# A fused kernel's last stage by 512 tokens, with its output products five feature blocks behind

## The chip, the core and the metric

The program runs on one core of a Trainium2 chip. Five engines work in it, each through its own list of instructions in a fixed order: TensorE (PE, matmuls; PEld are its weight loads), VectorE (DVE), ScalarE (ACT), GpSimd (POOL) and SyncE (SP, which issues every DMA of this kernel). They wait for one another through semaphores. The metric is the device time of one execution, in microseconds. Before the change it is 1073.4 us (median of three runs, 1073.21 to 1075.92).

## What is computed

All inputs are float32, drawn with numpy (several arrive as float64 words and are decoded on the chip). Cut to what matters:

```python
# attention with a compressive memory, B, H, S, D = 4, 8, 576, 64
out = g * mem_out + (1 - g) * softmax(causal(q @ k.T / 8)) @ v
x = out.transpose(0, 2, 1, 3).reshape(2304, 512)
# first layer, 512 -> 2048 -> 512
h = x @ w_in
x = (h * tanh(log1p(exp(h)))) @ w_out
# second layer, 512 -> 1024 -> 1024 -> 512
a = x @ w1
b = x @ w2
result = (a * b @ w3) @ w_out2
```

## The kernel before

Every large product is kept near float32 precision by splitting each operand into a rounded high part and a low remainder and adding three products (high by high, high by low, low by high). So one logical product of a 128-row block is three matmuls per 128 rows of depth.

There are three parts. In the first, 16 pairs of heads go through attention. In the second, the first layer runs by quarters of its 2048 features (g = 0 to 3, in the code `emit_h` and `emit_x2`), each over eight units of 288 tokens; `x2` collects the result. While the quarters run, the weights of the second layer are decoded from their 64-bit words by `decode` (six DVE operations and one POOL addition per 128x512 block) and parked in DRAM. In the last quarter `fold()` multiplies w3 by w_out2 once, so that the second layer's two last products become one: for each of 8 row blocks it takes two half steps; a half step loads raw words (`draw`), decodes them into `da`, transposes them on PE (four 128x128 transposes, L597), has ACT and DVE split the transposed block into `w3h` and `w3l`, and adds twelve 128x512 matmuls in a `psF` bank. After the second half step ACT and DVE write the block out through `da` and `de`, and two DMAs put it in `w_dram` (L611, L612).

The third part is the stage that the change rewrites. It takes `x2` by 256 tokens (`T`), nine chunks. For each chunk, `emit_ab` does eight feature blocks: 12 matmuls for b, 12 for a, then ACT, DVE, ACT and DVE turn them into the split product of a and b in `pbuf`. `emit_out` of the chunk before follows: two blocks of 128 tokens, each 24 matmuls of 512 columns against the folded weight `wft`, an ACT copy and a DMA to the output. `wft` is read back from `w_dram` into the place of `o2` once the fold is done.

Two things set the order. The code emits fold steps between units by `steps(folding, 3)`, and a scheduler then orders the instructions of each engine by priority of emission and by its own timing, so that what is ready early fills gaps. Tiles of one tag share a fixed number of buffers, and a new tile gets its buffer when the old one's last reader is done; the eight PSUM banks are three `A`, three `X`, two `F`. The fold uses both `F` banks, one for the sum and one for the transposes. In the quarters `gh` and `gl` are the split activations that `emit_x2` reads.

Of the kernel before, what the change touches and what calls it, by code (L numbers as in the profile page):

```python
# [21 lines left out]
def fused_kernel(ctx: ExitStack, tc, q, k, v, M_prev, z_prev, beta, w_in, w_out, w1, w2, w3, w_out2, out):  # L22
# [23 lines left out]
    def psA():  # L46
        return bank("A")
# [35 lines left out]
    def decoder(stack, raw, n):  # L83
        dec.update(pool=stack.enter_context(tc.tile_pool(name="dec", bufs=1)), raw=raw, n=n)
# [369 lines left out]
    def emit_h(u):  # L454

        g, b, z = u
        t = wts[g]
        x = xl[b]
        cs = slice(CH * z, CH * z + CH)
        y = [wps[0].tile([128, 2, CH], F32, tag=f"y{i}", name="y", bufs=1) for i in range(2)]  # L460
        hp = []
        for m in range(KQ):
            o = bank(HU.get(u, HT[g == NQ - 1])[m])[:, 0:CH]
            ms = slice(128 * m, 128 * m + 128)
            for kk in range(KD):
                mm(o, t[:, 0, kk, ms], x[:, 0, kk, cs], kk == 0, False)
                mm(o, t[:, 0, kk, ms], x[:, 1, kk, cs], False, False)
                mm(o, t[:, 1, kk, ms], x[:, 0, kk, cs], False, kk == KD - 1)
            hp.append(o)
        for m in range(KQ):  # L470
            nc.scalar.activation(out=y[m // 2][:, m % 2], in_=hp[m], func=AF.Tanh, scale=0.5)

        d = wps[0].tile([128, 1], F32, tag="dum", name="dum", bufs=2)
        first = nc.scalar.activation(out=d, in_=y[1][:, 1, 0:1], func=AF.Sin, scale=0.0)
        with tc.issue_after(first.ins):
            for i in range(2):
                nc.scalar.activation(out=y[i], in_=y[i], func=AF.Arctan, scale=-0.5, bias=half)
        gg = []
        for i in range(2):
            nc.scalar.activation(out=y[i], in_=y[i], func=AF.Sin, scale=-2.0, bias=halfpi)  # L480
            for j in range(2):
                nc.vector.tensor_tensor(out=y[i][:, j], in0=y[i][:, j], in1=hp[2 * i + j], op=ALU.mult)
            gh = wps[0].tile([128, 2, CH], F32R, tag="gh", name="gh", bufs=3)
            gl = wps[0].tile([128, 2, CH], F32R, tag="gl", name="gl", bufs=3)
            nc.scalar.copy(out=gh, in_=y[i])
            sub(gl, y[i], gh)
            gg.append((gh, gl))
        gt[u] = gg
# [133 lines left out]
    folding = fold()  # L622
    nextq = iter(())
    prev = None
    w1t, w2t, wft = [None, None], [None, None], [None]
    for u in [(g, b, z) for g in range(NQ) for b in range(B) for z in range(2)]:
        g, b, z = u
        last = g == NQ - 1
        if u not in gt:
            if last and fpool[0] is None:  # L630
                steps(nextq, 100)
                steps(pre, 100)
                dk.close()
                fpool[0] = fk.enter_context(tc.tile_pool(name="fp", bufs=1))
                decoder(fk, 1, 2)
            emit_h(u)
        if last:
            if z == 0 and b > 0:
                wt, wd = ((w1t, w1_dram), (w2t, w2_dram))[(b - 1) % 2]
                i = (b - 1) // 2  # L640
                wt[i] = w_slot(b - 1, "w12t")
                from_dram(wt[i], wd, slice(512 * i, 512 * i + 512))
            if b > 0:
                steps(folding, 3)
        if prev is not None:
            emit_x2(prev)
        if not last:
            if b == 0 and z == 0:
                nextq = load_quarter(g + 1)
            steps(nextq, 2)  # L650
            steps(pre, 1)
        prev = u
# [6 lines left out]


    wp3 = ctx.enter_context(tc.tile_pool(name="wp3", bufs=1, side="right"))
    T = 256
    NM = FF2 // 128
    pp = {}
    late = [None]
    pbuf = w2q[0].tile([128, 2, 2, NM, T], F32R, tag="wq1", name="pbuf")

    def emit_ab(c):
        xh = wp3.tile([128, KD, T], F32R, tag=f"x2h{c % 2}", name="x2h", bufs=1)
        xlo = (wp3 if c % 2 == 0 or c < 3 else late[0]).tile([128, KD, T], F32R, tag="x2l", name="x2l", bufs=1)  # L670
        s = x2[:, :, T * c:T * c + T]
        nc.scalar.copy(out=xh, in_=s)
        sub(xlo, s, xh)
        t = pbuf[:, c % 2]
        pp[c] = t
        for m in range(NM):
            pa, pb = psA()[:, 0:T], psA()[:, 0:T]
            m2 = slice(128 * (m % 4), 128 * (m % 4) + 128)
            for o, w, cs in ((pb, w2t[m // 4], m2), (pa, w1t[m // 4], m2)):
                for kk in range(KD):  # L680
                    mm(o, w[:, 0, kk, cs], xh[:, kk], kk == 0, False)
                    mm(o, w[:, 0, kk, cs], xlo[:, kk], False, False)
                    mm(o, w[:, 1, kk, cs], xh[:, kk], False, kk == KD - 1)
            bs = wp3.tile([128, T], F32, tag="bs", name="bs", bufs=2)
            nc.scalar.copy(out=bs, in_=pb)
            nc.vector.tensor_tensor(out=bs, in0=bs, in1=pa, op=ALU.mult)  # L686
            nc.scalar.copy(out=t[:, 0, m], in_=bs)  # L687
            sub(t[:, 1, m], bs, t[:, 0, m])
            if c < 2:
                steps(folding, 1)  # L690

    def emit_out(c):
        t = pp.pop(c)
        for i in range(T // 128):
            o = psX()
            ts = slice(128 * i, 128 * i + 128)
            for m in range(NM):
                w = wft[0][:, :, 4 * (m // 4):4 * (m // 4) + 4]
                mm(o, t[:, 0, m, ts], w[:, 0, m % 4], m == 0, False)
                mm(o, t[:, 0, m, ts], w[:, 1, m % 4], False, False)  # L700
                mm(o, t[:, 1, m, ts], w[:, 0, m % 4], False, m == NM - 1)
            ob = wp3.tile([128, DM], F32, tag="ob", name="ob", bufs=2)
            nc.scalar.copy(out=ob, in_=o)
            r0 = T * c + 128 * i
            dm(out=out[r0:r0 + 128, :], in_=ob)

    NC = NT // T
    for c in range(NC):
        emit_ab(c)
        if c == 1:  # L710
            steps(folding, 100)
            fk.close()
            late[0] = ctx.enter_context(tc.tile_pool(name="late", bufs=1))
            wft[0] = wq.tile([128, 2, NM, DM], F32R, tag="wq0", name="wft")
            for i in range(2):
                for s in range(2):
                    dm(
                        out=f(wft[0][:, i, 4 * s:4 * s + 4]),
                        in_=w_dram[i, 512 * s:512 * s + 512, :].rearrange("(k p) f -> p k f", p=128),
                    )  # L720
        if c > 0:
            emit_out(c - 1)
    emit_out(NC - 1)


# [30 lines left out]
```

## Time and profile before

| | |
|---|---|
| Median of the runs | 1073.4 us |
| The profiled execution: its own time / its span | 1075.49 us / 1073.7 us |
| PE busy | 1023.7 us, 95% |
| DVE, ACT, POOL busy | 63%, 51%, 36% |
| Mean granted clock of PE | 0.991 of full speed |
| Chain of work that ended last | PE 62%, DVE 20%, POOL 7%, DMA 6% |

The span is what the profiler saw of one execution; the execution's own time lies 1.8 us above it. An engine's busy share is an average over very different parts. PE is idle for some 34 us in the first 300 us, and close to always busy after that; so in the rest of the program a stretch of time is worth what PE has to do in it, plus what PE waits. In timeline rows the columns are start, length, engine, line, operation, output and inputs with their sizes, the count and, in brackets, the idle time before it and who ended it. Lengths of matmuls overlap, since they are pipelined: the pace is read from starts, or from a long run of them.

### The profile page before, as it was taken

How to read it: one execution, taken by the hardware profiler on the slowest of the kernel's cores; microseconds unless marked ns; L12 is line 12 of the kernel's file. 1: busy time of each engine (PE TensorE's matmuls, PEld its weight loads, DVE VectorE, ACT ScalarE, POOL GpSimd, SP SyncE). 2: the span in 40 equal slices, each digit the busy share in tenths (PEclk: the TensorE clock that was granted, in tenths of full speed). 3: DMA queues.
4: the chain of work that ended last, by engine and by line, in shares of the span. 5: the costliest groups of instructions: out<-in, count | busy, mean ns of one | idle time of the engine just before them, and what ended most of it. 6: DMA issues, size and time to landing. Idle time of an engine off the chain costs nothing.

```text
span 1073.7 us, 19071 instructions
## 1 busy us (share of the span) xinstructions
PE 1023.7 (95%) x7128; PEld 913.2 (85%) x7128; DVE 671.9 (63%) x1563; ACT 548.0 (51%) x1157; POOL 387.3 (36%) x377
## 2 busy tenths in 40 slices
PE   6998898899998999999999999999999999999998
PEld 5665655567798999999999999999998999999997
DVE  6699999896689888888987535647551122222220
ACT  5776767677765666666666655653231222222221
POOL 7668898784255556555555001010100000000000
PEclk9999999999999999999999999999999999999999
DMA  6788777675233343333332264323115100000001
GB/s 149 167 188 188 186 181 184 169 187 117 79 98 101 112 161 109 109 130 127 118 99 101 63 243 146 136 89 128 62 58 176 40 5 17 20 21 16 6 20 40
DMA packets 111341, 116.70 MB, mean 109 GB/s; under 512 B 71696, under 2 KB 73744, under 8 KB 111248
## 3 DMA queue, kind: packets, MB, share of 16 engines
q1 hardware_dynamic: 111248, 115.48, 37.6%
q8 instruction: 56, 0.92, 0.4%
q14 instruction: 37, 0.30, 0.1%
HBM read 71.83 MB, written 21.50 MB: 87 GB/s over the span
## 4 chain that ended last, share of the span: by engine, by line
PE 62%; DVE 20%; POOL 7%; DMA 6%; issue 3%; SPq 1%; ACT 0%; DVEq 0%; POOLq 0%; ACTq 0%
PE psA L59 28%; PE psX L59 24%; PE psF L59 6%; DVE de L104 3%; POOL da L120 2%; DVE da L102 2%; PE psF L426 2%; DVE de L103 2%; DVE s L361 2%; DVE da L99 2%; POOL da L105 2%; DVE da L98 2%; DVE da L100 2%; DMA w_dram<-da 1%; DVE s L356 1%
## 5 line engine op out<-in xcount | busy, mean ns | idle before, releaser
L105 POOL TENSOR_TENSOR da<-da,de 128x512 f32<-128x512 f32 x72 | 100.1, 1395 | 336.0 <-DVE de L104 272.6
L59 PE MATMUL psX<-gh,wqt 128*128 128x288 f32 x1024 | 209.0, 298 | 9.9 <-DVE x L575 5.4
L59 PE MATMUL psA<-x2h,w12t 128*128 128x256 f32 x1152 | 210.4, 283 | 0.0
L59 PEld LDWEIGHTS psA<-x2h,w12t 128*128 128x128 f32 x1152 | 180.8, 192 | 1.0
L59 PEld LDWEIGHTS psX<-gh,wqt 128*128 128x128 f32 x1024 | 164.6, 188 | 13.5 <-DVE x L575 6.7
L59 PE MATMUL psA<-x2l,w12t 128*128 128x256 f32 x576 | 163.2, 284 | 0.4 <-DVE x2l L65 0.4
L59 PE MATMUL psX<-gl,wqt 128*128 128x288 f32 x512 | 150.9, 295 | 0.0
L686 DVE TENSOR_TENSOR bs<-bs,psA 128x256 f32<-128x256 f32 x72 | 30.3, 421 | 161.5 <-PE psA L59 156.8
L59 PE MATMUL psA<-xt,wqt 128*128 128x288 f32 x840 | 119.9, 296 | 0.0
L59 PEld LDWEIGHTS psA<-xt,wqt 128*128 128x128 f32 x840 | 115.0, 189 | 2.3 <-issue 1.0
L59 PEld LDWEIGHTS psA<-x2l,w12t 128*128 128x128 f32 x576 | 110.3, 192 | 1.4 <-DVE x2l L65 0.7
L366 ACT ACTIVATE s<-s,acc 128x512 f32<-128x512 f32 (+4 forms) x144 | 84.2, 587 | 39.7 <-DVE acc L361 34.2
L59 PE MATMUL psX<-wft,pbuf 128*128 128x512 f32 x432 | 101.7, 394 | 2.3 <-DMA wft<-w_dram 2.3
L59 PEld LDWEIGHTS psX<-wft,pbuf 128*128 128x128 f32 x432 | 81.4, 190 | 19.3 <-DMA wft<-w_dram 2.8
L59 PEld LDWEIGHTS psX<-gl,wqt 128*128 128x128 f32 x512 | 96.5, 189 | 0.2
L687 ACT CAST pbuf<-bs 128x256 fp32r<-128x256 f32 x72 | 29.3, 406 | 110.4 <-DVE bs L686 97.3
L98 DVE TENSOR_SCALAR da<-draw 128x512 int32<-128x512 int32 x72 | 44.1, 616 | 61.5 <-DMA draw<-in_moe_w_dram 23.1
L59 PE MATMUL psF<-xt,wqt 128*128 128x288 f32 x552 | 77.3, 295 | 0.0
L426 PE MATMUL psF<-ident,s 128*128 128x128 f32 x400 | 67.7, 283 | 10.0 <-DVE s L356 6.6
L59 PE MATMUL psX<-pt,raw 128*64 128x64 f32 (+4 forms) x576 | 74.8, 329 | 0.0
L59 PEld LDWEIGHTS psF<-xt,wqt 128*128 128x128 f32 x552 | 74.5, 188 | 0.1
L361 DVE CUSTOM_DVE_ANT_0 s<-psA,mask 128x512 f32<-128x512 f32 (+3 forms) x144 | 64.2, 477 | 15.0 <-PE psA L59 11.0
(116 smaller groups left out, 1920.8 us busy)
## 6 DMA issues: line engine op xcount, KB each, us to landing
draw<-in_moe_w_dram SPq DMA_DIRECT2D x32, 512.0 KB, 3.7
draw<-in_moe_w_out_dram SPq DMA_DIRECT2D x24, 512.0 KB, 3.9
draw<-in_moe_w_in_dram SPq DMA_DIRECT2D x16, 512.0 KB, 4.4
w12t<-w_dram SPq DMA_DIRECT2D x8, 1024.0 KB, 7.8
w_dram<-de SPq DMA_DIRECT2D x24, 256.0 KB, 2.4
w_dram<-da SPq DMA_DIRECT2D x24, 256.0 KB, 2.4
out_dram<-ob SPq DMA_DIRECT2D x18, 256.0 KB, 2.0
eqk<-hl SPq DMA_DIRECT2D x30, 144.0 KB, 2.7
```

The lines of the kernel that those rows point to most:

```text
L59: nc.tensor.matmul(o, lhsT=l, rhs=r, start=start, stop=stop)
L98: V.tensor_scalar(out=ai, in0=hw, scalar1=0x7FFFFFFF, scalar2=None, op0=ALU.bitwise_and)
L99: V.tensor_scalar(out=a, in0=a, scalar1=2.0 ** -15, scalar2=122879.9921875, op0=ALU.max, op1=ALU.min)
L100: V.tensor_scalar(out=ai, in0=ai, scalar1=3, scalar2=0x3FFFFFF8, op0=ALU.logical_shift_left, op1=ALU.bitwise_and)
L102: V.scalar_tensor_tensor(out=ai, in0=hw, scalar=-0x40000000, in1=ai, op0=ALU.bitwise_and, op1=ALU.bitwise_or)
L104: V.scalar_tensor_tensor(out=e, in0=lw.bitcast(U32), scalar=2.0 ** -52, in1=e, op0=ALU.mult, op1=ALU.mult)
L105: nc.gpsimd.tensor_tensor(out=a, in0=a, in1=e, op=ALU.add)
L361: nc.vector.tensor_tensor_reduce(out=s, in0=o, in1=m, op0=ALU.add, op1=ALU.min, scale=-scale, scalar=init, accum_out=a,)
L366: nc.scalar.activation(out=s, in_=s, func=AF.Exp, scale=-1.0, bias=a, accum_out=r)
L426: nc.tensor.transpose(o[:, 128 * x:128 * x + 128], src[:, 128 * jb:128 * jb + 128], ident)
L686: nc.vector.tensor_tensor(out=bs, in0=bs, in1=pa, op=ALU.mult)
L687: nc.scalar.copy(out=t[:, 0, m], in_=bs)
```

## The change

The last stage takes 512 tokens at a time (four spans of 512 and one of 256). One feature block of `emit_ab` is now 24 matmuls of 512 columns. Its bank for a is `A` in even blocks and `F` in odd ones. The output products come one feature block at a time, five blocks behind (`LAG`), and add into four banks that stay open over a whole span (`X`, `X`, `X`, `F`). The products of a and b go through a ring of six blocks instead of `pbuf`. The fold gets two raw buffers in place of one, its steps begin one unit earlier in the last quarter, and the code asks for one more step in each of the first five blocks. `gh` and `gl` have two buffers in place of three. `wft` is loaded with the first 512 rows of both parts first.

```diff
-            gh = wps[0].tile([128, 2, CH], F32R, tag="gh", name="gh", bufs=3)
-            gl = wps[0].tile([128, 2, CH], F32R, tag="gl", name="gl", bufs=3)
+            gh = wps[0].tile([128, 2, CH], F32R, tag="gh", name="gh", bufs=2)
+            gl = wps[0].tile([128, 2, CH], F32R, tag="gl", name="gl", bufs=2)
...
-                decoder(fk, 1, 2)
+                decoder(fk, 2, 2)
...
-            if b > 0:
+            if (b, z) > (0, 0):
                 steps(folding, 3)
...
-    T = 256
+    T = 512
+    RING = 6
...
+    def emit_ab(k):
+        c, m = work[k]
+        n = spans[c][1]
+        x = xs_[c % 2]
+        pb, pa = (bank(t)[:, 0:n] for t in ("AA", "AF")[m % 2])
+        m2 = slice(128 * (m % 4), 128 * (m % 4) + 128)
+        for o, w in ((pb, w2t[m // 4]), (pa, w1t[m // 4])):
+            for kk in range(KD):
+                mm(o, w[:, 0, kk, m2], x[0][:, kk, 0:n], kk == 0, False)
+                mm(o, w[:, 0, kk, m2], x[1][:, kk, 0:n], False, False)
+                mm(o, w[:, 1, kk, m2], x[0][:, kk, 0:n], False, kk == KD - 1)
+        t = ring[:, k % RING]
+        bs = wp3.tile([128, T], F32, tag="bs", name="bs", bufs=1)[:, 0:n]
...
+        if m == 0:
+            outs[c] = [bank(tag) for tag in "XXXF"[0:n // 128]]
+        for i, o in enumerate(outs[c]):
+            ts = slice(128 * i, 128 * i + 128)
+            mm(o, t[:, 0, ts], wft[0][:, 0, m], m == 0, False)
+            mm(o, t[:, 0, ts], wft[0][:, 1, m], False, False)
+            mm(o, t[:, 1, ts], wft[0][:, 0, m], False, m == NM - 1)
...
+    LAG = RING - 1
+    split_x2(0)
+    for k, (c, m) in enumerate(work):
+        emit_ab(k)
+        if k < LAG:
+            steps(folding, 1)
+        if k == LAG - 1:
+            end_fold()
+        if m == 5 and c + 1 < len(spans):
+            split_x2(c + 1)
+        if k >= LAG:
+            emit_out(k - LAG)
```

How the instructions move is seen at three places. The first is PE in the fold's last part, before: `ident,da` is the name of a half step's transposes (they stand above this piece), `o,w3h` and `o,w3l` its products, `x2h` and `x2l` blocks of the last stage.

```order
L59 MATMUL psA<-x2l,w12t 128x256
L59 MATMUL psA<-x2h,w12t 128x256 x2
L59 MATMUL psA<-x2l,w12t 128x256
L59 MATMUL psA<-x2h,w12t 128x256 x2
L59 MATMUL psF<-o_7976,w3h 128x512 x2
L59 MATMUL psA<-x2l,w12t 128x256
L59 MATMUL psA<-x2h,w12t 128x256 x2
L59 MATMUL psA<-x2l,w12t 128x256
L59 MATMUL psA<-x2h,w12t 128x256
L59 MATMUL psF<-o_7976,w3l 128x512
L59 MATMUL psF<-o_7976,w3h 128x512 x2
```

Between the transposes and the first product stand 26 matmuls of the last stage, and five or more between the first products with `w3h` and the first with `w3l`. The same engine and place in the changed kernel (`room` holds the low part of x2):

```order
L59 MATMUL psA<-room,w12t 128x512
L59 MATMUL psA<-x2h,w12t 128x512
L597 MATMUL psF<-ident,da 128x128 x4
L59 MATMUL psF<-o_7841,w3h 128x512 x2
L59 MATMUL psF<-o_7841,w3l 128x512
L59 MATMUL psF<-o_7841,w3h 128x512 x2
L59 MATMUL psF<-o_7841,w3l 128x512
L59 MATMUL psF<-o_7841,w3h 128x512 x2
L59 MATMUL psF<-o_7841,w3l 128x512
L59 MATMUL psF<-o_7841,w3h 128x512 x2
L59 MATMUL psF<-o_7841,w3l 128x512
L597 MATMUL psF<-ident,da 128x128 x4
```

The last four of the 16 half steps now stand one straight behind another, with nothing of the last stage between; the 72 matmuls that the three `A` banks can take stand ahead of them, and 36 more with `F` banks behind them.

The second place is DVE at the same stretch. Before, the last half step's words are decoded like this (`bs`, `pbuf` belong to the last stage):

```order
L98 TENSOR_SCALAR da_9179<-draw_9177 128x512
L99 TENSOR_SCALAR da_9179<-da_9179 128x512
L100 TENSOR_SCALAR da_9179<-da_9179 128x512
L102 SCALAR_TENSOR_TENSOR da_9179<-draw_9177,da_9179 128x512
L686 TENSOR_TENSOR bs_9803<-bs_9803,psA_9777 128x256
L65 TENSOR_TENSOR w3l_9025<-psF_9026,w3h_9024 128x512
L103 TENSOR_SCALAR de_9180<-da_9179 128x512
L65 TENSOR_TENSOR pbuf_9334<-bs_9803,pbuf_9334 128x256
L104 SCALAR_TENSOR_TENSOR de_9180<-draw_9177,de_9180 128x512
```

And in the changed kernel, from the split of the last but two half step (`w3l_8851`) on; `de_8872` writes out row block 6, `da_8880` and `da_9047` are the words of the last two half steps:

```order
L65 TENSOR_TENSOR w3l_8851<-psF_8852,w3h_8850 128x512
L98 TENSOR_SCALAR da_8880<-draw_8878 128x512
L99 TENSOR_SCALAR da_8880<-da_8880 128x512
L610 TENSOR_TENSOR de_8872<-psF_8806,da_8871 128x512
L100 TENSOR_SCALAR da_8880<-da_8880 128x512
L102 SCALAR_TENSOR_TENSOR da_8880<-draw_8878,da_8880 128x512
L98 TENSOR_SCALAR da_9047<-draw_9045 128x512
L103 TENSOR_SCALAR de_8881<-da_8880 128x512
L99 TENSOR_SCALAR da_9047<-da_9047 128x512
L104 SCALAR_TENSOR_TENSOR de_8881<-draw_8878,de_8881 128x512
L100 TENSOR_SCALAR da_9047<-da_9047 128x512
```

Two half steps are decoded in turn now. The writing out of block 6 stands inside the decoding of `da_8880`, and so does the first operation on `da_9047`, whose buffer is the one that `da_8871` leaves when its DMA to DRAM is done.

The third place is DVE in quarter 1, one unit of 288 tokens, before (`x2` with `psX` is what `emit_x2` adds up, `gl` the low part of the activations):

```order
L577 TENSOR_TENSOR x2_3941<-x2_3941,psX_6318 128x288
L482 TENSOR_TENSOR y_6229<-y_6229,psF_6256 128x288
L482 TENSOR_TENSOR y_6229<-y_6229,psF_6269 128x288
L65 TENSOR_TENSOR gl_6294<-y_6228,gh_6293 128x576
L577 TENSOR_TENSOR x2_3941<-x2_3941,psX_6332 128x288
L65 TENSOR_TENSOR gl_6301<-y_6229,gh_6300 128x576
L577 TENSOR_TENSOR x2_3941<-x2_3941,psX_6346 128x288
```

and after:

```order
L577 TENSOR_TENSOR x2_3941<-x2_3941,psX_6318 128x288
L482 TENSOR_TENSOR y_6229<-y_6229,psF_6256 128x288
L482 TENSOR_TENSOR y_6229<-y_6229,psF_6269 128x288
L577 TENSOR_TENSOR x2_3941<-x2_3941,psX_6332 128x288
L98 TENSOR_SCALAR da_6510<-draw_6508 128x512
L99 TENSOR_SCALAR da_6510<-da_6510 128x512
L65 TENSOR_TENSOR gl_6294<-y_6228,gh_6293 128x576
L577 TENSOR_TENSOR x2_3941<-x2_3941,psX_6346 128x288
```

The first `gl` moved behind the third addition into x2, and the second behind the fourth, into the stretch of decoding that stands ahead of the next unit's first addition.

## Rows read from the trace of the kernel before

**Rows 1.** The page: busy us (share) xinstructions, and PE's granted clock in 40 slices.

```profile
PE 1023.7 (95%) x7128; PEld 913.2 (85%) x7128; DVE 671.9 (63%) x1563; ACT 548.0 (51%) x1157; POOL 387.3 (36%) x377
...
PEclk9999999999999999999999999999999999999999
```

**Rows 2.** PE's waits from 730 to 860: us in total, times, longest us.

```profile
PE psX L59 <- DMA wft<-w_dram: 2.3, 1, 2.3
PE psA L59 <- DVE x2l L65: 0.4, 1, 0.4
```

**Rows 3.** The chain that ended last: start us, us, what; one chunk.

```profile
855.54 23.03 PE psA L59 x192
878.58 10.91 PE psX L59 x48
```

**Rows 4.** Timeline of PE behind its wait for the folded weight.

```profile
819.75 9.20 PE L59 MATMUL psX<-wft,pbuf 128*128 128x512 f32 x33 [2.35 <-DMA wft<-w_dram]
```

**Rows 5.** Windows of 1 us: busy by engine, granted clock, DMA share, GB/s.

```profile
819.00:820.00 1.00, 0.25 (x1) 0.25 (x2) 0.00 (x0) 0.00 (x0) 0.00 (x0) 0.72 0.98 375
...
822.00:823.00 1.00, 1.00 (x4) 0.77 (x3) 0.00 (x0) 0.00 (x0) 0.00 (x0) 0.57 0.75 231
```

**Rows 6.** Timeline, one half step of the fold and its writing out.

```profile
735.46 0.60 PE L597 MATMUL psF<-ident,da 128*128 128x128 f32 x4
735.82 0.38 PE L59 MATMUL psX<-gh,wqt 128*128 128x288 f32 x1
736.10 0.59 ACT L599 CAST w3h<-psF 128x512 fp32r<-128x512 f32 x1 [7.44 <-PE psF L597]
736.73 0.68 DVE L65 TENSOR_TENSOR w3l<-psF,w3h 128x512 fp32r<-128x512 f32 x1
737.76 0.63 PE L59 MATMUL psF<-o,w3h 128*128 128x512 f32 x2
740.52 0.52 PE L59 MATMUL psA<-x2h,w12t 128*128 128x256 f32 x3
740.77 0.59 ACT L609 CAST da<-psF 128x512 fp32r<-128x512 f32 x1 [0.81 <-issue]
```

**Rows 7.** Timeline, decoding of a block on DVE and POOL.

```profile
748.30 0.43 DVE L98 TENSOR_SCALAR da<-draw 128x512 int32<-128x512 int32 x1 [0.43 <-DMA draw<-in_moe_w_dram]
748.76 0.43 DVE L99 TENSOR_SCALAR da<-da 128x512 f32<-128x512 f32 x1
751.90 0.69 DVE L104 SCALAR_TENSOR_TENSOR de<-draw,de 128x512 f32<-128x512 uint32 x1
752.72 1.30 POOL L105 TENSOR_TENSOR da<-da,de 128x512 f32<-128x512 f32 x1 [6.42 <-issue]
```

**Rows 8.** DMA issues from 735 to 850: KB each, median us to landing.

```profile
w_dram<-da SPq DMA_DIRECT2D x4, 256.0 KB, 2.2
```

**Rows 9.** Timeline, the last product of the fold and the issue of the folded weight.

```profile
810.21 0.39 PE L59 MATMUL psF<-o,w3l 128*128 128x512 f32 x1
...
810.63 0.92 SPq L717 DMA_DIRECT2D wft<-w_dram  x2
```

**Rows 10.** Timeline, activations of one unit in quarter 1.

```profile
425.13 0.67 ACT L485 CAST gh<-y 128x576 fp32r<-128x576 f32 x1 [0.28 <-DVE y L482]
...
426.45 3.36 PE L59 MATMUL psA<-xt,wqt 128*128 128x288 f32 x24
...
429.84 0.75 DVE L65 TENSOR_TENSOR gl<-y,gh 128x576 fp32r<-128x576 f32 x1
...
432.85 0.43 PE L59 MATMUL psX<-gh,wqt 128*128 128x288 f32 x2
```

**Rows 11.** PE's waits from 300 to 600.

```profile
PE psX L59 <- DVE x L575: 5.4, 4, 2.3
PE psX L59 <- DVE x L577: 4.3, 4, 2.1
```

**Rows 12.** Timeline of the end: the last copy on ACT.

```profile
1070.14 0.59 ACT L703 COPY ob<-psX 128x512 f32<-128x512 f32 x1 [4.85 <-PE psX L59]
```

More of the change, by code (lines that the diff above doesn't have):

```diff
@@ L661, in fused_kernel @@
     wp3 = ctx.enter_context(tc.tile_pool(name="wp3", bufs=1, side="right"))
-    T = 256
+    T = 512
     NM = FF2 // 128
[L664 to L695, printed above, removed]
-            ts = slice(128 * i, 128 * i + 128)
[L697 to L722, printed above, removed]
@@ L723, in fused_kernel, with end_fold @@
-    emit_out(NC - 1)
+    RING = 6
+    wft = [None]
+    room = w2q[0].tile([128, 2 * RING + KD, T], F32R, tag="wq1", name="room")
+    ring = room[:, 0:2 * RING].rearrange("p (r i) t -> p r i t", i=2)
+    xs_ = {0: (wp3.tile([128, KD, T], F32R, name="x2h"), room[:, 2 * RING:])}
+    def end_fold():
+        steps(folding, 100)
+        fk.close()
+        late = ctx.enter_context(tc.tile_pool(name="late", bufs=1))
+        x = late.tile([128, 2, KD, T], F32R, name="x2s")
+        xs_[1] = (x[:, 0], x[:, 1])
+        wft[0] = wq.tile([128, 2, NM, DM], F32R, tag="wq0", name="wft")
+        for s in range(2):
+            for i in range(2):
+                dm(
+                    out=f(wft[0][:, i, 4 * s:4 * s + 4]),
+                    in_=w_dram[i, 512 * s:512 * s + 512, :].rearrange("(k p) f -> p k f", p=128),
+                )
@@ new lines, in fused_kernel, with split_x2 @@
+    spans = [(t, min(T, NT - t)) for t in range(0, NT, T)]
+    work = [(c, m) for c in range(len(spans)) for m in range(NM)]
+    outs = {}
+    def split_x2(c):
+        t0, n = spans[c]
+        x = xs_[c % 2]
+        for kk in range(KD):
+            s = x2[:, kk, t0:t0 + n]
+            nc.scalar.copy(out=x[0][:, kk, 0:n], in_=s)
+            sub(x[1][:, kk, 0:n], s, x[0][:, kk, 0:n])
+    def emit_ab(k):
+        c, m = work[k]
+        n = spans[c][1]
+        x = xs_[c % 2]
+        pb, pa = (bank(t)[:, 0:n] for t in ("AA", "AF")[m % 2])
+        m2 = slice(128 * (m % 4), 128 * (m % 4) + 128)
+        for o, w in ((pb, w2t[m // 4]), (pa, w1t[m // 4])):
+            for kk in range(KD):
+                mm(o, w[:, 0, kk, m2], x[0][:, kk, 0:n], kk == 0, False)
[3 more added lines that the diff above has]
+        bs = wp3.tile([128, T], F32, tag="bs", name="bs", bufs=1)[:, 0:n]
+        nc.scalar.copy(out=bs, in_=pb)
+        nc.vector.tensor_tensor(out=bs, in0=bs, in1=pa, op=ALU.mult)
+        nc.scalar.copy(out=t[:, 0, 0:n], in_=bs)
+        sub(t[:, 1, 0:n], bs, t[:, 0, 0:n])
@@ new lines, in emit_out @@
+    def emit_out(k):
+        c, m = work[k]
+        t0, n = spans[c]
+        t = ring[:, k % RING]
+        if m == 0:
+            outs[c] = [bank(tag) for tag in "XXXF"[0:n // 128]]
+        for i, o in enumerate(outs[c]):
+            ts = slice(128 * i, 128 * i + 128)
+            mm(o, t[:, 0, ts], wft[0][:, 0, m], m == 0, False)
+            mm(o, t[:, 0, ts], wft[0][:, 1, m], False, False)
+            mm(o, t[:, 1, ts], wft[0][:, 0, m], False, m == NM - 1)
+            if m == NM - 1:
+                ob = wp3.tile([128, DM], F32, tag="ob", name="ob", bufs=2)
+                nc.scalar.copy(out=ob, in_=o)
+                dm(out=out[t0 + 128 * i:t0 + 128 * i + 128, :], in_=ob)
@@ L727 @@
+    LAG = RING - 1
[10 more added lines that the diff above has]
+            emit_out(k - LAG)
+    for k in range(len(work) - LAG, len(work)):
+        emit_out(k)
 _INS = ['q', 'k', 'v', 'M_prev', 'z_prev', 'beta', 'moe_w_in', 'moe_w_out',
```

2 lines of the change are left out of this document (1 added, 1 removed).

## Prediction

> **What bounds the kernel now.** I read the page first, then PE's waits in the stretch that the change rewrites, then the chain of waits, the timeline and the windows there. The page shows PE busy for 95% of the span, with a granted clock of 0.9 or more in every slice [rows 1]. The reader is to see that no other engine comes near: DVE, second, has 63%. From 730 us to 860 us PE waits twice in all, 2.3 us for the folded weight `wft` and 0.4 us for a split of x2 [rows 2]. So the last 330 us are PE's work and little else, and the sum below is PE's: what it has to issue, plus what it waits, plus what it loses to a lower clock. The chain gives the pace: 192 matmuls of 256 columns take 23.03 us, 119.9 ns each, and 48 of 512 columns take 10.91 us, 227.3 ns each [rows 3].
>
> **The width.** Before, nine chunks of 192 matmuls at 119.9 ns are 207.3 us. After, four spans of 192 at 227.3 ns are 174.6 us and the last, 256 wide, is 23.0 us: 197.6 us, a gain of 9.7 us. The 432 output matmuls are 512 wide in both kernels and cost the same in either order. The nearest other row for a 512-wide matmul is the fold's: twelve from 737.76 to 740.52 are 230 ns each [rows 6], which would leave 7.6 us of gain. I take 9.7, from the steady run.
>
> [...]
>
> **What goes.** [...] With the 0.4 us for x2, which four smaller pieces remove, 4.4 us would go. What is late next is `wft` again, below.
>
> **What comes: four half steps of the fold without cover.** The calls for fold steps in the first five blocks do nothing: seven units ask for three each, 21, and the generator is exhausted after 16, as it was before (six units, 18). All fold work is thus emitted ahead of the last stage, and block 1 needs an `F` bank that the fold holds until its end. The order shows the consequence: 72 matmuls that fit into three `A` banks, then four half steps back to back. PE takes its list in order, so it waits inside each. A half step from the start of its transposes [rows 6]: ACT starts at +0.64 and takes 0.59, so the first product can go at about +1.27; DVE follows ACT and is done at +1.95, so the third product, the first that reads `w3l`, can go at +2.0. PE fills 0.36 (transposes, the next row starts at 735.82) and 0.46 (two products) of it: 1.18 us of waiting, 4.7 us for four. Before, 26 matmuls covered it at no cost.
>
> The third of the four waits much longer. Its words are decoded in turn with those of the fourth, and the writing out of row block 6 stands among them. From the end of the second half step's last product, PE has nothing else to do until this: ACT writes block 6 from +0.25 to +0.84 [rows 6]; its DMA lands 2.2 us later, +3.05 [rows 8]; only then may DVE start on `da_9047`, which gets that buffer; three operations of 0.46 and one of 0.69 (L98, L103, L99, L104) end at +5.1, POOL starts 0.13 later and takes 1.30 [rows 7], and PE gets its transposes at about +6.6. Queued behind them on PE are two half steps and the whole last stage; on DVE the rest of the decoding. I bound this hole by 6.2 (the DMA at 2.0, POOL at 1.28) and 7.4 us.
>
> A wait of 2.35 us brought the clock down in rows 4 and 5, so this one does too. The half step behind it has twelve products: at the lower level throughout they cost 2.7 us more, over half of them 1.4. I take 2.0, and 0 to 3.5 as its bounds. The fourth half step's words are ready by then (they end some 2.3 us behind the third's).
>
> **`wft` after the change.** It is issued behind the fold's last product, as before: the product starts at 810.21, 0.23 us later the next can go, SP issues at 810.63 [rows 9], and PE resumes at 819.75 [rows 4], 9.3 us behind the product. Now 36 matmuls of 227.3 ns and one output product stand in between, 8.4 us. A wait of 0.9 us is left; the clock falling there as well would be 1.7 more. The second half of `wft` has three more blocks, over 20 us.
>
> **Edits at nothing.** Two `gh` buffers: a cast that now waits for the unit before starts at about 425.6 instead of 425.13, six of the 24 matmuls of 0.14 us ahead of 426.45; its `gl` would follow, but the next products start at 432.85 and the last `gl` is done at 430.59 [rows 10], so 2.3 us cover the 0.5; without that cover it is 0.5 us in each of 24 units, 12 us. Four open output banks: the next span's first product comes 24 matmuls, 5.5 us, behind the last copy's start, and a copy takes 0.59 [rows 12]. Raw buffers: the fold gets one half step further ahead of the last stage, which is the same work at another time. At the end two copies stand 0.7 us apart instead of 5.4; a copy of 0.59 fits, 0.1.
>
> **The sum.** Against the profiled execution, 1075.5 us (span 1073.7, 1.8 around it): -9.7 - 4.4 + 4.7 + 6.6 + 2.0 + 0.9 + 0.1 = +0.2, 1075.7. The median of the runs shown lies 2.1 below that execution, so I forecast 1073.6 us: no change that can be told. With the bounds (gain 7.6 to 9.7, hole 6.2 to 7.4, clock 0 to 3.5, `wft` 0 to 2.6) this case reaches from 1070.3 to 1079.7, and most of it from 1071.5 to 1077.
>
> **Rivals.** *Faster: the quarters lose their waits.* PE waits eight times, 9.7 us, for an addition into x2 that frees an `X` bank [rows 11]. The order puts the first `gl` behind the third addition, so later banks come free earlier. Against it: the same order puts a `gl` ahead of the next unit's first addition, which is the one that is late when DVE is behind. Half of the waits gone would give 1068.8, all 1064. Chance 0.22.
>
> *Slower: the clock stays down.* [...] Chance 0.22.
>
> *Slower: two `gh` buffers are too few.* If `gl` is late in every unit of three quarters, 12 us: 1086. Against it the 2.3 us of cover. Chance 0.04.
>
> *The width does nothing,* because a 512-wide product of x2 costs two 256-wide ones: 1083. Rows 3 speak against it. Chance 0.02.
>
> *The open banks bring the clock down.* If each of five spans costs one fall, 1.7 us apiece as in rows 4: 1082. The rows that speak on it are the granted clock's last slices, where banks take turns as well and it stays at 0.9 or more [rows 1]. Chance 0.02. [...]
>
> **How the numbers follow.** A measurement of this kernel tells about 0.3%, 3.2 us, from no change. My forecast has 0.48, the faster rival 0.22, the slower ones 0.30. The forecast's own spread gives a few hundredths to either side, and weak forms of the rivals fall within the bound: faster 0.24, same 0.46, slower 0.30. The range of 8 in 10 takes in half of the faster rival and the slower clock: 1068.5 to 1080.
>
> **What would show it.** Right: in the last stage, blocks of 24 matmuls in 5.5 us; four half steps with gaps of about 1.2 us; one gap of 6 to 7 us on PE that ends with transposes released by POOL, with a row of a lower clock behind it; `wft` waited for by under 2 us. Wrong: that gap under 4 us (then the sum is 2 to 4 us faster), 512-wide matmuls at 240 ns, or waits on `psX` in the quarters that differ from 9.7 us by more than 3.

## The result, and the profile after

The changed kernel takes 1085.16 us (median of 4 runs, 1083.02 to 1086.68) against 1074.12 us for the kernel before, measured beside it: ratio 1.0099, 95% interval 1.0076 to 1.0123, 11 us slower. The forecast of no change (1073.6 us, range to 1080) is wrong.

The last stage, on which nearly the whole prediction was spent, came out as forecast. The chain that ended last, after (start us, us, what):

```profile
837.76 5.44 PE psA L59 x24
```

A block of 24 matmuls of 512 columns takes 5.44 us, 226.7 ns each (the forecast's pace was 227.3). PE's waits from 740 to 860 us, after (us in total, times, longest):

```profile
PE psF L597 <- POOL da L105: 6.0, 1, 6.0
PE psF L59 <- ACT w3h L599: 2.7, 4, 0.7
```

Where [rows 2] showed one wait for `wft` there are now the four uncovered half steps and the one long hole. The timeline of PE at the first and the third of these half steps, after:

```profile
775.85 0.60 PE L597 MATMUL psF<-ident,da 128*128 128x128 f32 x4
777.12 0.73 PE L59 MATMUL psF<-o,w3h 128*128 128x512 f32 x2 [0.68 <-ACT w3h L599]
777.85 0.51 PE L59 MATMUL psF<-o,w3l 128*128 128x512 f32 x1
...
780.26 0.60 PE L597 MATMUL psF<-ident,da 128*128 128x128 f32 x4
...
784.42 0.39 PE L59 MATMUL psF<-o,w3l 128*128 128x512 f32 x1
790.82 1.12 PE L597 MATMUL psF<-ident,da 128*128 128x128 f32 x4 [6.01 <-POOL da L105]
792.61 1.22 PE L59 MATMUL psF<-o,w3h 128*128 128x512 f32 x2 [0.68 <-ACT w3h L599]
...
797.86 0.60 PE L597 MATMUL psF<-ident,da 128*128 128x128 f32 x4
```

The products start 1.27 us behind the transposes and the first with `w3l` 2.00 us behind them, as worked out. Behind the hole the twelve products take 5.25 us (792.61 to 797.86) against 3.14 us in the first half step (777.12 to 780.26, the next transposes): the granted clock had fallen, as the windows of that stretch show (columns as in [rows 5]; the last two are of 1 us).

```profile
780.00:790.00 10.00, 4.14 (x18) 2.59 (x16) 5.53 (x12) 1.17 (x2) 0.52 (x1) 0.88 0.14 52
790.00:800.00 10.00, 7.83 (x23) 5.49 (x24) 3.82 (x5) 1.17 (x2) 2.04 (x2) 0.61 0.01 3
...
797.00:798.00 1.00, 1.00 (x5) 0.69 (x4) 0.00 (x0) 0.00 (x0) 0.00 (x0) 0.60 0.00 0
798.00:799.00 1.00, 0.46 (x5) 0.22 (x3) 0.00 (x0) 0.50 (x1) 0.00 (x0) 1.00 0.00 0
```

So the 11 us are not there. They are in the quarters. PE's waits from 300 to 600 us, after, answer to [rows 11]:

```profile
PE psX L59 <- DVE x L575: 8.7, 8, 2.5
PE psX L59 <- DVE x L577: 8.4, 7, 2.3
PE psX L59 <- DVE gl L65: 1.3, 2, 0.6
```

18.4 us in place of 9.7, and 17.1 of them are for VectorE's additions. So the next view is VectorE over the same work in both kernels: from the first addition into x2 to the 96th, which ends quarter 2. The window of that stretch before (the third pair is VectorE's busy time):

```profile
304.90:616.80 311.90, 302.06 (x2240) 299.39 (x2241) 260.21 (x507) 197.77 (x308) 160.78 (x133) 0.99 0.35 114
```

VectorE's groups by line and shape in it, before (busy us, mean ns, idle before):

```profile
L65 DVE TENSOR_TENSOR gl<-y,gh 128x576 fp32r<-128x576 f32 x48 | 45.1, 940 | 2.1 <-ACT gh L485 2.0
L104 DVE SCALAR_TENSOR_TENSOR de<-draw,de 128x512 f32<-128x512 uint32 x45 | 36.8, 831 | 0.4
L102 DVE SCALAR_TENSOR_TENSOR da<-draw,da 128x512 int32<-128x512 int32 x44 | 30.3, 701 | 0.1
L577 DVE TENSOR_TENSOR x<-x,psX 128x288 f32<-128x288 f32 x64 | 28.4, 443 | 3.0 <-PE psX L59 3.0
```

The same stretch of work after, as a window:

```profile
305.30:627.70 322.40, 304.12 (x2231) 299.85 (x2232) 267.29 (x505) 191.93 (x305) 154.85 (x133) 0.99 0.35 111
```

And its groups, after:

```profile
L104 DVE SCALAR_TENSOR_TENSOR de<-draw,de 128x512 f32<-128x512 uint32 x45 | 39.7, 892 | 0.5
L65 DVE TENSOR_TENSOR gl<-y,gh 128x576 fp32r<-128x576 f32 x47 | 39.5, 842 | 1.5 <-ACT gh L485 1.5
L102 DVE SCALAR_TENSOR_TENSOR da<-draw,da 128x512 int32<-128x512 int32 x44 | 38.5, 885 | 0.4
L577 DVE TENSOR_TENSOR x<-x,psX 128x288 f32<-128x288 f32 x63 | 27.9, 443 | 4.1 <-PE psX L59 4.1
```

The same work takes 10.5 us longer. Outside this stretch the two profiled executions agree: 304.9 and 305.3 us ahead of it, 456.9 and 457.2 us behind it. VectorE is busy 7.1 us longer with the same kinds of instructions: one L102 takes 885 ns in place of 701, an addition keeps its 443 ns, and a `gl` is even shorter, 842 for 940. VectorE's listed waits in the stretch sum to 50.1 us before and 52.9 after, so they did not take up the longer work; with them 310.3 of 311.9 us and 320.2 of 322.4 are accounted for.

The chain that ended last passes through the same stretch like this, before and after (shares of the stretch):

```profile
by line: PE psX L59 14.4%; PE psA L59 9.0%; POOL da L120 7.6%; issue 7.3%; DVE de L104 7.0%; POOL da L105 5.7%; DVE de L103 5.2%; PE psF L59 5.1%; DMA w_dram<-da 5.0%; DVE da L102 4.7%; DVE da L99 4.2%; POOL de L62 3.8%; DVE da L100 3.6%; D
...
by line: issue 13.5%; DMA w_dram<-da 9.6%; DVE de L104 8.6%; DVE da L102 8.5%; PE psX L59 6.5%; DVE da L98 6.1%; DVE de L103 6.0%; DVE gl L65 5.6%; DVE da L99 4.6%; DVE da L100 4.1%; DMA o_dram<-da 3.7%; PE psA L59 3.3%; POOL da L105 3.2%; 
```

The decoding is on it in both kernels: VectorE's operations, GpSimd's, and the write `w_dram<-da`, whose buffer the next decoding needs. After, L102 and that write have about doubled their shares, and PE's products have lost more than half of theirs.

What makes VectorE's instructions longer shows when VectorE and GpSimd are laid side by side. Before, around one unit of quarter 1 (VectorE's and GpSimd's rows in order of start):

```profile
434.30 0.68 DVE L102 SCALAR_TENSOR_TENSOR da<-draw,da 128x512 int32<-128x512 int32 x1
434.53 1.61 POOL L105 TENSOR_TENSOR da<-da,de 128x512 f32<-128x512 f32 x1 [4.89 <-DVE de L104]
435.02 1.41 DVE L103 TENSOR_SCALAR de<-da 128x512 int32<-128x512 int32 x1
...
436.46 0.98 DVE L104 SCALAR_TENSOR_TENSOR de<-draw,de 128x512 f32<-128x512 uint32 x1
437.37 0.44 DVE L577 TENSOR_TENSOR x<-x,psX 128x288 f32<-128x288 f32 x1
437.53 1.29 POOL L105 TENSOR_TENSOR da<-da,de 128x512 f32<-128x512 f32 x1 [0.62 <-DVE de L104]
```

And after, the same place:

```profile
437.89 0.68 DVE L104 SCALAR_TENSOR_TENSOR de<-draw,de 128x512 f32<-128x512 uint32 x1
438.49 0.42 DVE L100 TENSOR_SCALAR da<-da 128x512 int32<-128x512 int32 x1
438.71 1.34 POOL L105 TENSOR_TENSOR da<-da,de 128x512 f32<-128x512 f32 x1 [5.14 <-DVE de L104]
438.94 1.67 DVE L102 SCALAR_TENSOR_TENSOR da<-draw,da 128x512 int32<-128x512 int32 x1
440.15 0.94 POOL L62 TENSOR_SCALAR wqt<-da 128x512 fp32r<-128x512 f32 x1
440.64 0.72 DVE L103 TENSOR_SCALAR de<-da 128x512 int32<-128x512 int32 x1
441.17 1.34 POOL L65 TENSOR_TENSOR wqt<-da,wqt 128x512 fp32r<-128x512 f32 x1
441.40 1.65 DVE L104 SCALAR_TENSOR_TENSOR de<-draw,de 128x512 f32<-128x512 uint32 x1
...
443.13 1.28 POOL L105 TENSOR_TENSOR da<-da,de 128x512 f32<-128x512 f32 x1 [0.63 <-DVE de L104]
443.34 1.35 DVE L98 TENSOR_SCALAR da<-draw 128x512 int32<-128x512 int32 x1
```

An L102 that starts 0.23 us behind a GpSimd addition ends 0.56 us behind that addition's end, and takes 1.67 us in place of 0.68. After, the two decodings of a unit are further apart when the first one's L104 lets GpSimd start, so three operations of the second (L102, L103, L104), and L98 of the next, each start beside a GpSimd operation. Before, GpSimd starts one operation later in the second decoding: its L102 started first and kept its 0.68 us, two operations are held up (L103, L104), and more of GpSimd's work falls beside additions from PSUM, which keep their 0.44 us. Counted from 300 to 600 us, 1 of 45 L102 starts while GpSimd works before and 9 of 44 after; of L103 it is 9 and 15, and of `gl`, which moved the other way, 29 of 44 and 12 of 43. In exchange GpSimd has become 5.9 us less busy in the stretch (160.78 to 154.85, the fifth pair).

### The profile page after: what moved, and what is told of

Same layout as the page of the kernel before. It is cut to its first block, busy times and chain, and to the rows that moved or that the text cites. A ratio compares the mean times of both kernels' runs of the same rounds, so it can differ in the third digit from the quotient of the medians.

```text
span 1084.9 us, 17371 instructions
## 1 busy us (share of the span) xinstructions
PE 1022.4 (94%) x6360; PEld 878.7 (81%) x6360; DVE 674.8 (62%) x1510; ACT 534.7 (49%) x1104; POOL 381.4 (35%) x377
## 4 chain that ended last, share of the span: by engine, by line
PE 54%; DVE 25%; DMA 7%; issue 5%; POOL 5%; SPq 2%; ACT 1%; DVEq 0%; POOLq 0%; ACTq 0%
PE psA L59 21%; PE psX L59 18%; PE psF L59 11%; DVE da L102 3%; DMA w_dram<-da 3%; DVE de L104 3%; DVE da L98 2%; DVE de L103 2%; DVE s L361 2%; DVE da L99 2%; PE psF L426 2%; DVE da L100 2%; DVE gl L65 2%; DVE s L356 2%; POOL wqt L65 1%
## 5 line engine op out<-in xcount | busy, mean ns | idle before, releaser
L59 PE MATMUL psX<-gh,wqt 128*128 128x288 f32 x1024 | 209.9, 298 | 17.1 <-DVE x L575 8.7
L105 POOL TENSOR_TENSOR da<-da,de 128x512 f32<-128x512 f32 x72 | 100.3, 1395 | 330.2 <-DVE de L104 301.3
L59 PE MATMUL psX<-wft,room 128*128 128x512 f32 x336 | 82.2, 390 | 0.0
L711 ACT COPY bs<-psA 128x512 f32<-128x512 f32 (+1 forms) x40 | 21.8, 546 | 121.1 <-PE psA L59 115.7
L59 PE MATMUL psA<-x2h,w12t 128*128 128x512 f32 (+1 forms) x288 | 79.7, 354 | 0.0
L485 ACT CAST gh<-y 128x576 fp32r<-128x576 f32 x64 | 43.2, 675 | 70.0 <-PE psX L59 38.3
L98 DVE TENSOR_SCALAR da<-draw 128x512 int32<-128x512 int32 x72 | 44.7, 626 | 50.4 <-DMA w_dram<-da 21.1
L59 PEld LDWEIGHTS psX<-wft,room 128*128 128x128 f32 x336 | 62.6, 188 | 12.6
L712 DVE TENSOR_TENSOR bs<-bs,psA 128x512 f32<-128x512 f32 (+1 forms) x20 | 12.7, 634 | 93.3 <-PE psA L59 91.9
L428 ACT COPY pt<-psF 128x512 f32<-128x512 f32 (+1 forms) x112 | 57.2, 541 | 26.7 <-PE psF L426 26.1
L426 PEld LDWEIGHTS psF<-ident,s 128*128 128x128 f32 x400 | 49.4, 148 | 25.7 <-DVE s L356 6.5
```

What stands on the lines that cost most here:

```text
L59: nc.tensor.matmul(o, lhsT=l, rhs=r, start=start, stop=stop)
L98: V.tensor_scalar(out=ai, in0=hw, scalar1=0x7FFFFFFF, scalar2=None, op0=ALU.bitwise_and)
L105: nc.gpsimd.tensor_tensor(out=a, in0=a, in1=e, op=ALU.add)
L426: nc.tensor.transpose(o[:, 128 * x:128 * x + 128], src[:, 128 * jb:128 * jb + 128], ident)
L428: nc.scalar.copy(out=t[:, 0:n], in_=o[:, 0:n])
```

## The experiments

The times are medians, and the ratios are to the kernel before, measured beside each group. The first group asked which part of the change costs the time. Theory A is the two `gh` buffers, theory B the earlier and doubled loading of raw words.

**Two buffers alone in the kernel before.**

```diff
-            gh = wps[0].tile([128, 2, CH], F32R, tag="gh", name="gh", bufs=3)
+            gh = wps[0].tile([128, 2, CH], F32R, tag="gh", name="gh", bufs=2)
```

(and `gl` alike)

> The kernel before with two buffers for gh and gl instead of three, nothing else. Theory A (the two buffers alone slow the quarters): the loss between 300 and 600 us comes here too, about 11 to 13 us, so 1084 to 1087 us, with PE's waits on x2 additions at 16 us or more instead of 9.7 and ACT waiting for gl some 45 us instead of 7. Rival B (the two raw buffers and the fold that starts a unit earlier slow the quarters): this kernel stays at 1074 us.

Measured: 1085.18 us, 1.0110 [1.0062, 1.0158]. The one edit costs as much as the whole change, 1085.18 against 1085.16. The interval alone would leave some 5 us for the rest of the change, but the traces narrow it: behind the 96th addition both executions take 457.2 us, and the kernel before 456.9.

**Three buffers in the changed kernel**, with one raw buffer, for which there is space then (`decoder(fk, 1, 2)`).

> The changed kernel with three buffers for gh and gl and one raw buffer (three and two do not fit together). Theory A: the quarters are as before, the last stage gains its width and loses it in the uncovered half steps, so 1072 to 1076 us. Rival C (the last stage by 512 tokens loses by itself, the quarters are incidental): 1083 us or more.

Measured: 1080.63 us, 1.0062 [1.0042, 1.0083], above the 1072 to 1076 of theory A. The quarters are nearly as before (the 96 additions take 313.4 us, PE's waits for additions 11.2), and the loss lies behind them: 462.7 us from the 96th addition to the end, in place of 456.9. There, with one raw buffer, the last stage has two holes, 7.5 us, in place of one, and two waits for `w3l`, 2.1 us.

**Blocks of the last stage between the half steps:** the odd ones of the first five blocks take a free `X` bank for a, not an `F` bank.

```diff
-        pb, pa = (bank(t)[:, 0:n] for t in ("AA", "AF")[m % 2])
+        pb, pa = (bank(t)[:, 0:n] for t in ("AX" if k < LAG and m % 2 else ("AA", "AF")[m % 2]))
```

> The changed kernel, but in the first five blocks the odd ones take an X bank for a instead of an F bank, so that they need not wait for the fold. Theory A with the hole as read: the hole of 6 us and two of the four short ones are covered, but only 12 matmuls stand ahead of the first use of wft, which then waits about 6 us: about 3 us faster than the changed kernel, 1081 to 1084 us, and PE's 6 us wait for POOL gone. Rival D (the holes are hidden time that comes back elsewhere): no change, 1085 us.

Measured: 1079.47 us, 1.0043 [1.0020, 1.0067], 5.7 us below the changed kernel and 1.5 below its range. The 6.0 us hole is gone and a wait of 3.0 us for `wft` takes part of it back.

**Both edits together.**

> Both edits together: three buffers for gh and gl, one raw buffer, X banks for a in the early odd blocks. Theory A: the sum of the two, 1068 to 1073 us, the fastest of the four. Rival B: as slow as the changed kernel in the quarters, 1080 us or more.

Measured: 1075.01 us, 1.0006 [0.9982, 1.0029], 2 us above its range: the two gains add up (4.5 and 5.7 us below the changed kernel, together 10.2), but with one raw buffer a hole of 3.1 us stays.

The second group asked how two buffers cost 11 us. Theory C: the cast waits for its buffer. Theory L: a late `gl` holds the single `y`, for which the next unit's tanh waits. Theory D: `gl` stands behind a decoding operation that waits for a DMA.

**A second y buffer** (`bufs=2` for `y`, two `gh` buffers).

> The kernel before with gh and gl in two buffers (as in the first experiment, 1085.2 us) and the activations' scratch tile y in two buffers instead of one. DVE's order is the same as there. Theory L (the late low part gl is paid for through y: the next unit's first ScalarE operation L471 must not overwrite y before gl has read it, so its MULs, the x2 additions and PE's X banks come late): the wait of L471 for gl, 49 us there from 300 to 600 us, goes, PE's waits for L575 and L577 there fall from 17 to about 10 us, and the time is about 1075 to 1077. Theory C (the cast itself waits for its buffer, and PE then waits for products whose operands come late whatever y does): y has no part in it, 1084 to 1087, PE's waits as there. Theory D (the place of gl behind a decoding operation on DVE that waits for a DMA holds up the additions that stand behind it on DVE): also 1083 to 1087, since DVE's order stays.

Measured: 1086.19 us, 1.0101 [1.0077, 1.0125]. ScalarE's 49 us of waiting for `gl` (300 to 600 us, in the first experiment) all but vanished, to 2.4, and the time stayed: that wait, the largest new one in the profile, cost nothing measurable. L falls. VectorE's row is not quite that of the first experiment, though the expectation took it to be: in the first half of the stretch `gl` stands earlier in many units.

**A third buffer for decoded words** (`decoder(dk, 2, 3)`, two `gh` buffers).

> The kernel before with gh and gl in two buffers and a third buffer for the words that the quarters decode (da, de), so that the first decoding operation L98 need not wait for the write to DRAM of the block two before. Theory D (L98's wait for that write, 19 us on DVE from 300 to 600 us with two gh buffers, holds gl and the additions): that wait falls to under 4 us, the wait of L471 for gl by more than half, and the time is 1075 to 1079. Theory C (the buffer wait of the cast alone): 1084 to 1087. Theory L alone, with gl late because it now stands behind decoding work of some us in any case: most of the loss stays, 1081 to 1085.

Measured: 1104.72 us, 1.0283 [1.0256, 1.0309]. From 300 to 600 us L98's wait for the write to `w_dram` fell from 19.4 us with two buffers alone to 1.6, and the kernel is 20 us slower still. D falls in this form, and this miss gave the theory that held. VectorE in the same stretch of work, with the third buffer:

```profile
309.20:648.40 339.20, 313.89 (x2231) 309.42 (x2232) 281.30 (x501) 192.07 (x303) 156.24 (x131) 0.95 0.32 102
```

And two of its groups there:

```profile
L102 DVE SCALAR_TENSOR_TENSOR da<-draw,da 128x512 int32<-128x512 int32 x44 | 39.0, 887 | 0.5
...
L99 DVE TENSOR_SCALAR da<-da 128x512 f32<-128x512 f32 x43 | 29.0, 675 | 0.5
```

VectorE is busy 281.3 us for work that took 260.2 before. L99, at 484 ns in the kernel before, is stretched as well: from 300 to 600 us 21 of 43 start while GpSimd works, in place of 4 of 44. Longer instructions need not be the whole of this loss, since PE's granted clock also fell in the stretch, to 0.95.

**Three buffers, but `gl` behind the third or fourth addition.**

```diff
...
+            for i, a in enumerate(lows):
+                with tc.issue_after(adds[i - 2].ins):
+                    sub(*a)
```

> The kernel before with its three gh buffers, but with each gl of the quarters put on DVE behind the third or fourth addition into x2, where the changed kernel has it. No cast waits for a buffer, only the order on DVE is that of the change. Theories L and D (what costs is where gl stands on DVE): the loss comes without the missing buffer, 1082 to 1087, with L471 waiting for gl for some 40 us from 300 to 600 us. Theory C (what costs is the cast's wait for its buffer): 1073 to 1076, with L471 waiting for gl 7 to 15 us.

Measured: 1074.59 us, 0.9989 [0.9970, 1.0009]. Moving `gl` alone costs nothing. That speaks for C, or for a row in which more than `gl` moves: L102 stayed at 713 ns here (300 to 600 us). `gl` was not as late as with two buffers either: ScalarE's L473 (L471 before the edit) waited 18.5 us for it, between the figures of the two theories.

**The changed kernel with a third buffer in quarters 0 to 2**, taken from space that the last quarter gives up, and with the `X` banks of the third experiment.

```diff
+            if own_third and turn[0] % 3 == 2:
+                gh = third[0].tile([128, 2, CH], F32R, tag="gh", name="gh", bufs=1)
...
+    third[0] = dk.enter_context(tc.tile_pool(name="third", bufs=1))
```

> The changed kernel with a third gh and gl buffer in quarters 0 to 2 only (in the space of the quarters' decoding, which the last quarter gives up anyway), with both raw buffers, and with the a banks of the odd blocks among the first five taken from X in place of F, so that PE has blocks of the last stage to do while the fold's last half steps wait. All theories agree on the quarters: DVE's order there is that of the kernel before, the 11 us come back, PE's waits for L575 and L577 from 300 to 600 us fall from 17 to about 10 us. With the last stage as in the third experiment (5.7 us below the changed kernel): 1067 to 1071. If the last stage does not keep that gain once the quarters run as before, because the fold then reaches it at another phase: 1073 to 1076.

Measured: 1065.43 us (1062.51 to 1067.15), 0.9906 [0.9884, 0.9928]. That is 1.6 us below its range. It beats both kernels, the one before by 9.3 us and the changed one by 19.7; in its profile the 96 additions take 308.8 us in place of 322.4, and what follows them 450.7 in place of 457.2.

The third group put theory C against theory P: the row of VectorE's instructions decides, because it sets which of them run beside GpSimd. The row of the quarters (from the first addition to the 96th, decoding included) was tied by edges from each instruction to the next:

```diff
...
+    for k in row:
+        ins = seen[k][at[k]].ins
+        at[k] += 1
+        if first is not None:
+            tc.add_manual_dep(ins, first.name, edge, reason="row")
+        first = ins
```

**Three buffers in the row of two.**

> The kernel before with its three gh and gl buffers, but with VectorE's instructions of quarters 0 to 2 (from the first addition into x2 to the 96th) tied to the row in which the kernel with two buffers has them, the decoding operations too. No cast waits for a buffer. Theory P (the row is what costs: in it the two decodings of a unit run staggered, so that GpSimd's addition L105 for the first falls beside decoding operations of the second, which then take 1.2 to 1.7 us in place of 0.4 to 0.7, where in the other row it falls beside additions from PSUM, which keep their 0.44 us; VectorE has no slack there): 1082 to 1087, L102 at 0.85 to 0.9 us on average in place of 0.69, busy time of VectorE from the first to the 96th addition some 6 us longer. Theory C (the cast's wait for its buffer is what costs): 1073 to 1076.

Measured: 1084.71 us, 1.0094 [1.0065, 1.0123]. The same stretch of work:

```profile
307.50:629.60 322.10, 305.32 (x2242) 301.35 (x2243) 267.51 (x506) 194.03 (x308) 154.82 (x133) 0.99 0.35 110
```

And the group that was stretched, there:

```profile
L102 DVE SCALAR_TENSOR_TENSOR da<-draw,da 128x512 int32<-128x512 int32 x44 | 38.6, 885 | 0.5
```

**Two buffers in the row of three.**

> The other half: the kernel before with two gh and gl buffers, VectorE's instructions of quarters 0 to 2 tied to the row that the kernel with three buffers has. Theory P alone: 1073 to 1078, since L102 is back at 0.69 us. Theory C alone: 1084 to 1088. There is a third way: gl now stands ahead of the unit's third addition and its cast waits for the end of the fourth block's products, which come after it; then VectorE stands still for 2 to 4 us in each of 22 units and the time is far above, 1100 to 1150, and the missing buffer does cost, but by way of the row that the scheduler chose to avoid just this.

Measured: 1073.49 us, 0.9995 [0.9973, 1.0016]. The same stretch:

```profile
307.00:616.80 309.80, 301.85 (x2238) 297.81 (x2239) 259.98 (x506) 196.16 (x305) 160.41 (x133) 1.00 0.35 114
```

And two groups of it:

```profile
L65 DVE TENSOR_TENSOR gl<-y,gh 128x576 fp32r<-128x576 f32 x48 | 44.2, 921 | 8.3 <-ACT gh L485 7.9 <-PE psX L59 0.4
...
L102 DVE SCALAR_TENSOR_TENSOR da<-draw,da 128x512 int32<-128x512 int32 x44 | 30.2, 700 | 0.1
```

With the two kernels above, that is a table of two by two:

| | row of three buffers | row of two buffers |
|---|---|---|
| three buffers | 1074.4 (before) | 1084.7 |
| two buffers | 1073.5 | 1085.2 |

(The 1085.2 is from the first group, where the kernel before had 1074.75.) The time goes with the row and not with the buffers. In the traces VectorE's row in the stretch is the same in both kernels of each column. GpSimd's row is as well, but it differs between the columns: with the row of two buffers GpSimd more often finishes one block before it starts the next addition. So the row that costs is VectorE's with the one of GpSimd that follows from it. Two buffers in the good row make VectorE wait 7.9 us for casts in 310 us, and it costs nothing measurable. The third way in that expectation, 2 to 4 us in each unit, did not come. C falls.

**GpSimd's L105 and L120 cut to 32 of 512 columns, in either row** (three buffers; the other columns are left out).

```diff
-        nc.gpsimd.tensor_tensor(out=a, in0=a, in1=e, op=ALU.add)
+        nc.gpsimd.tensor_tensor(out=a[:, 0:32], in0=a[:, 0:32], in1=e[:, 0:32], op=ALU.add)
```

(and L120, the subtraction, alike)

> Three gh buffers, VectorE's row of the kernel before tied, and GpSimd's two operations of the decoding, the addition L105 and the subtraction L120, cut to 32 of 512 columns (the other columns are left out, so the low parts of decoded weights are missing there). It is the yardstick for the next run. Theory P: VectorE loses its stretched instructions, L98 to L104 fall towards 0.42 and 0.69 us each, and the quarters come faster by up to the 8 us that they are stretched by from 300 to 600 us: 1064 to 1073. Theory C: no change but for shorter decoding chains, 1072 to 1075.

> The same short GpSimd operations (the same columns left out) with three buffers and VectorE tied to the row of the kernel with two. Against the run with the row of the kernel before: theory P expects the gap of about 11 us to shrink to 0 to 4 us, because what stretched VectorE's decoding is mostly gone. If the row costs by itself (gl late, additions late) and not by GpSimd, the gap stays at 8 to 12 us.

Measured: 1058.62 us (1056.93 to 1060.66) in the row of three buffers, 1059.34 us (1058.57 to 1061.05) in the row of two. The first came 5 us below its range, and the gap shrank from 10.3 to 0.7 us. The window of the same stretch, in the row of three:

```profile
305.10:603.50 298.40, 298.28 (x2243) 297.81 (x2242) 231.23 (x507) 199.84 (x309) 84.28 (x133) 1.00 0.38 119
```

And in the row of two:

```profile
304.60:603.30 298.70, 298.58 (x2246) 298.11 (x2245) 236.22 (x507) 199.52 (x309) 85.03 (x133) 1.00 0.38 119
```

L102 in the two, in the same order:

```profile
L102 DVE SCALAR_TENSOR_TENSOR da<-draw,da 128x512 int32<-128x512 int32 x44 | 30.1, 696 | 0.1
...
L102 DVE SCALAR_TENSOR_TENSOR da<-draw,da 128x512 int32<-128x512 int32 x44 | 30.7, 708 | 0.5
```

This shows what stretches it: in the same row of two, but with GpSimd's operations short, L102 is at 708 ns in place of 885, and VectorE is 29 to 31 us less busy than with full ones. The shrunken gap shows less. PE bounds the quarters now (it is busy in all but 0.1 us of either stretch), so any cost of the row on VectorE is hidden, and there is one: VectorE is still 5.0 us busier in the row of two (GpSimd's L62 and L65 are full length), with no effect on the time. That the row's cost is mostly stretched instructions rests on the busy times: 7.3 of the 10.2 us by which the work took longer with three buffers in the row of two. The rest is in VectorE's waits, which I did not separate.

## Why the prediction was wrong

**The step that failed** is the first of "Edits at nothing": "Two `gh` buffers", where 2.3 us of cover were set against a wait of 0.5 us. That this wait would cost nothing was right, since two buffers in the old row took 1073.5 us. But the edit also changes the row that the scheduler writes for VectorE. The third order excerpt showed it, `gl` moved in among L98 and L99, and I priced that move at nothing without laying the new row beside GpSimd. It cost 10.3 us by itself (three buffers in the row of two). One of the prediction's own signs of being wrong came true by it: the waits on `psX` in the quarters differ from 9.7 us by 8.7.

**The durations were taken where nothing stood beside them.** [rows 7] give L98 and L99 0.43 us and L104 0.69, all while GpSimd was idle. The trace of before already held stretched ones: L103 at 1.41 us beside L105, and a mean of 831 ns for L104. Laying the starts and lengths of VectorE's operations from 300 to 600 us against GpSimd's in the changed kernel: L102 takes 0.68 us clear of GpSimd and 1.24 where it overlaps with it (16 of 44), 1.67 for the nine of them that start while GpSimd works; the additions take 0.44 to 0.45 either way. Single rows show the same: the L102 at 438.94, with two inputs in SBUF, ends 0.56 us behind the end of L105; before, the L105 at 434.53, which started 0.23 us behind an L102, took 1.61 us, against 1.29 for the one at 437.53; and additions with one input in PSUM keep 0.44. L103, with one input in SBUF, is held up too: 1.41 us at 435.02 (before), against 0.42 clear of GpSimd. The stretched rows of before spoke against a row which sets decoding beside GpSimd, and I did not weigh them.

**What bounds the quarters.** From the page I read that no other engine comes near PE [rows 1]. VectorE's 63% is a mean over the program. In the stretch above it was 83% (260.2 of 311.9 us), and the decoding that VectorE shares with GpSimd and the writes to DRAM was on the chain that ended last already before the change. There the stretched instructions came out in the time: 7.1 us more of work went with 10.5 us more of time.

**The rivals.** "Two `gh` buffers are too few" named the edit and nearly the time (1086, chance 0.04), which is luck, since the runs refute its path: neither the cast's wait nor `gl`'s lateness costs by itself. "Faster: the quarters lose their waits" saw the same move in the row and expected a gain from it; the waits of 9.7 us became 18.4.

**The rest of the sum held.** From the 96th addition to the end the changed kernel takes 457.2 us and the one before 456.9, so it is +0.3 us, against +0.2. Its terms: the width's pace 226.7 ns for 227.3; the half steps at +1.27 and +2.00 us as worked out (the first takes 4.41 us in all, some 0.1 more than its terms); the hole 6.2 us (from 784.65, when the next matmul could go, to 790.82) for 6.6, at its lower bound; the clock about 2.6 us for 2.0, since the transposes behind the hole run slowly too (1.79 us to the first product in place of 1.27); and no wait for `wft` at all, for 0.9. The 2.0 was an estimate between 1.4 and 2.7 us, which take the lower clock as half of the full one; windows of 1 us show it at 0.50 from 788 to 797 us. No run shows the 4.4 us of "What goes" by themselves: 2.3 and 0.4 are the waits of [rows 2], and 1.7 is an estimate, the 9.20 us of [rows 4] less 33 times the 227.3 ns of [rows 3], in a stretch where the granted clock was 0.50 (820 to 822 us, before). The changed kernel has neither wait from 740 to 860 us, and its clock is 1.00 from 800 to 860. The clock did not stay down: in the windows of 1 us above it is back when the fourth half step begins (797.86), whose products take 3.1 us.

## What to carry to other kernels

Where a scheduler writes the order, the price of one buffer fewer is not the wait that it adds but the new row: lay that row beside the engines that can hold it up before pricing it at nothing. Take an instruction's duration from a place where its neighbours are those that it will have, and compare the mean of a group with its shortest row: a mean well above it says that something stretches it (L104 here: 831 ns against 0.68 us). The longest new wait in a profile may cost nothing (49 us on ScalarE here), so the share of the chain that ended last is worth reading beside the waits; tying a row and keeping the buffers, and the other way round, told cause from symptom in two runs.

## What the runs showed of the hardware

A VectorE operation of 0.42 us on SBUF alone (L103, one input) took 1.41 us beside a GpSimd addition, so one-input operations of the decoding are held up as well, not only those with two inputs (L102: 1.67 us in place of 0.68). The order of VectorE's instructions, with the same work and the same buffers, was worth 10.3 us of 1074. A third buffer for decoded words, which cut VectorE's waits for one DMA from 19.4 to 1.6 us, came with a kernel 20 us slower, in which more decoding starts beside GpSimd (L99: 21 of 43, in place of 4 of 44 before). And a wait of 6.2 us on PE went with a mean granted clock of 0.61 over the 10 us that begin near its end, yet this lower clock cost only about 2.6 us.
